# Tiles of x loaded from the Pool queue, weights loaded earlier, and memory columns copied one chain later, in a kernel of attention with recurrent memory plus a mixer MLP

## The chip, the cores and the metric

The kernel runs on one core of one Trainium2 chip. The metric is the device time of one execution in microseconds, as a median over several executions.

Ratios are the mean time of one kernel's fast runs over the mean time of the other's fast runs in the same rounds, so they are not quite the ratio of the medians that are quoted. They come with a 95% interval. Several chips were used: only kernels of one call share a chip and the runs of the kernel before.

## The reference, cut to what matters

Two branches read the same layer-normalised input, and the result is `x + A + B`.

```python
x = A_x                                     # (1, 2048, 1024), bf16
xn = _layernorm(x, axis=-1)
return x + _A_ref(xn, A_mem0, A_Wq, A_Wk, A_Wv, A_Wo, 32) + _B_ref(xn, B_w1, B_w2, B_w3, B_w4)

# A: for each of 64 segments of 32 tokens: 8 memory rows and the segment give q, k, v (32 heads of 128),
#    masked softmax, output projection; the first 8 output rows are the memory of the next segment
# B: h = gelu(layernorm(x) @ w1); four quarters of h shifted by -1, +1, -2, +2 tokens
#    x1 = x + shifted(h) @ w2 ;  x1 + gelu(layernorm(x1) @ w3) @ w4        # w3: 1024x3584
```

## The kernel before: the parts that matter

The kernel runs through stages one after another. Times are from its profile.

1. 0 to 72 us, "stage 1": 16 tiles of x (128 tokens each, 256 KB) are loaded, their statistics taken on VectorE, normalised, transposed (tiles 0 to 3 on TensorE, the others by a DMA transpose), and multiplied with w1. From tile 4 on two tiles are done at a time, with matmuls of 256 columns.
2. 72 to 127 us, the mixer: the product with w2, second layer norm, and a DMA transpose for each tile.
3. 127 to 531 us, the MLP: w3, gelu, w4, four times.
4. 531 us to the end: attention in 32 steps (4 blocks of 512 tokens, 8 groups of 4 heads). A step has 12 chains of 8 matmuls (4 for q, 4 for k, 4 for v). Work for the previous step's softmax is hooked between the chains.

Loads of x in stage 1. `nc.sync` is the SyncE queue, `nc.gpsimd` the Pool queue:

```python
def load_x(n):
    nc.sync.dma_start(xts[n][:], x_v[:, n, :])
...
load_x(0); load_x(1); load_w1(0); load_w1(2); load_x(2); load_w1(4); load_w1(6)   # (joined here)
for n in range(3, 8):
    load_x(n)
...
def ln_half(n, c):
    ...                                          # statistics on VectorE, then on Pool:
    nc.gpsimd.tensor_tensor(lnst[:, n, 2:4], ab[:], neghalf[:], op=ALU.pow)
...
def dma_trans(n):
    nc.sync.dma_start_transpose(xn2Ts[n // 2][:, n % 2, :, :], xn2s.pop(n)[:])
    if n + 4 < NT:
        load_x(n + 4)
    ...
def pe_trans(n):                                 # 8 matmuls with the identity, 2 copies on ScalarE
    ...
```

The part of attention that the change touches. `psO` is a buffer of two banks in PSUM, the memory that the matmuls write to. VectorE reads most of it (into `oX`), ScalarE the one memory column of each segment (into `oTm`):

```python
def values(s, m):
    ps = aux_tile([P, 4, 256], "B", "psO")
    for hh in range(4):
        nc.tensor.matmul(ps[:, hh, 0:TW], s.V[:, m, hh * P:(hh + 1) * P], BD[:, hh, :], start=True, stop=True)
    ...
    nc.vector.tensor_tensor(oX[...], p4[:, :, j0:4, 0:SEG], VM[...], op=ALU.add)
    nc.scalar.copy(oTm[:, hsl(s.hg), z:z + 4], p4[:, :, :, SEG])

for m in range(3):
    at(3 * m + 3, scores, p, m + 1)
    at(3 * m + 4, values, p, m)                  # hooked after chain 4, 7, 10
```

Of the kernel before, what the change touches and what calls it, by code (L numbers as in the profile page):

```python
# [25 lines left out]
NT = S // P  # L26
# [6 lines left out]
SEG = 32  # L33
# [30 lines left out]
def kernel(  # L64
# [16 lines left out]
    nc = tc.nc  # L81
    x_v = A_x[0].rearrange("(n p) d -> p n d", p=P)
# [49 lines left out]
    def mm_tile(name):  # L132
        return psum.tile([P, 512], F32, tag="mm", bufs=4, name=name)

    def aux_tile(shape, tag, name):
        return psum.tile(shape, F32, tag=tag, bufs=1, name=name)
# [16 lines left out]
    def load_w3(i):  # L153
        h, k = divmod(i, KT)
        nc.sync.dma_start(w3h[h][:, k, :], w3_v[:, k, h * FH * P:(h + 1) * FH * P])
# [7 lines left out]
    with ExitStack() as keepx:  # L163
        keep = keepx.enter_context(tc.tile_pool(name="keep", bufs=1))
        w2_sb = keep.tile([P, KT, D], BF16)
        xts = [keep.tile([P, D], BF16, name=f"x{n}") for n in range(NT)]
# [3 lines left out]
        with ExitStack() as p0:  # L170
# [6 lines left out]
            nc.scalar.activation(pre[:], fill[:, 0:1], ACTF.Gelu_apprx_tanh)  # L177

            def load_x(n):
                nc.sync.dma_start(xts[n][:], x_v[:, n, :])  # L180

            def load_w1(k0):
                nc.sync.dma_start(w1_sb[:, k0:k0 + 2, :], w1_v[:, k0:k0 + 2, :])
# [5 lines left out]
            load_x(2)  # L189
            load_w1(4)  # L190
            load_w1(6)
            for n in range(3, 8):
                load_x(n)

            def warm(c):
                ps = aux_tile([P, 512], "A", "psW")
# [5 lines left out]
            def ln_half(n, c):  # L202
                if c == 0:
                    sts[n] = ring.tile([P, 2, 6], F32, tag="st", name="st")
                nc.vector.bn_stats(sts[n][:, c, :], xts[n][:, c * 512:(c + 1) * 512])  # L205
                if c == 0:
                    return
                nc.vector.bn_aggr(lnst[:, n, 0:2], sts.pop(n)[:])
                ab = ring.tile([P, 2], F32, tag="ab", name="ab")
                nc.vector.tensor_scalar(ab[:, 0:1], lnst[:, n, 1:2], EPS, None, op0=ALU.add)  # L210
                nc.vector.tensor_scalar(ab[:, 1:2], ab[:, 0:1], EPS, lnst[:, n, 1:2], op0=ALU.mult, op1=ALU.add)
                nc.gpsimd.tensor_tensor(lnst[:, n, 2:4], ab[:], neghalf[:], op=ALU.pow)

            def ln_stats(n):
                ln_half(n, 0)
                ln_half(n, 1)
# [13 lines left out]

            def dma_trans(n):
                nc.sync.dma_start_transpose(xn2Ts[n // 2][:, n % 2, :, :], xn2s.pop(n)[:])
                if n + 4 < NT:
                    load_x(n + 4)
                if n == 8:
                    nc.sync.dma_start(m0[:], A_mem0[0])
                if 8 <= n < 12:
                    kk = slice(2 * (n - 8), 2 * (n - 7))
                    nc.sync.dma_start(w2_sb[:, kk, :], w2_v[:, kk, :])
                elif n >= 12:  # L240
                    load_w3(n - 12)
# [4 lines left out]
            def pe_trans(n):  # L246
                xn2 = xn2s.pop(n)
                ps = [mm_tile("psT")[:], mm_tile("psT")[:]]
                for h in range(2):
                    p3_ = ps[h].rearrange("p (k t) -> p k t", k=4)  # L250
                    for k in range(4):
                        nc.tensor.matmul(p3_[:, k, :], xn2[:, (4 * h + k) * P:(4 * h + k + 1) * P], ident[:], start=True, stop=True)
                    for q in range(0, 4, 2 if n == 0 else 4):
                        w = 2 if n == 0 else 4
                        nc.scalar.copy(xn2Ts[n // 2][:, n % 2, 4 * h + q:4 * h + q + w, :], p3_[:, q:q + w, :])
# [70 lines left out]
            normalise_x(2)  # L326
            ln_stats(6)
            ln_apply(5)
            dma_trans(5)
            single(3, 1)  # L330
            normalise_x(3)
            for g in range(2, NT // 2):
# [19 lines left out]
        with ExitStack() as p2:  # L352
            ring = p2.enter_context(tc.tile_pool(name="p2ring", bufs=4))
            for n in range(NT):
                x1 = ring.tile([P, D], F32, tag="x1", bufs=6)
                st = ring.tile([P, 2, 6], F32, tag="st")
                for ch in range(2):
                    ps = mm_tile("ps2")
                    for k in range(KT):
                        o = 2 + n * P + SH[k]  # L360
                        nc.tensor.matmul(ps[:], hTB[:, k, o:o + P], w2_sb[:, k, ch * 512:(ch + 1) * 512], start=(k == 0), stop=(k == KT - 1))  # L361
                    nc.vector.tensor_tensor(x1[:, ch * 512:(ch + 1) * 512], ps[:], xts[n][:, ch * 512:(ch + 1) * 512], op=ALU.add)
                    nc.vector.bn_stats(st[:, ch, :], x1[:, ch * 512:(ch + 1) * 512])
                mv = ring.tile([P, 2], F32, tag="mv")
                nc.vector.bn_aggr(mv[:], st[:])
                a = ring.tile([P, 1], F32, tag="a")
                nc.gpsimd.tensor_scalar(a[:], mv[:, 1:2], EPS, None, op0=ALU.add)
                r3 = ring.tile([P, 1], F32, tag="r3")
                nc.gpsimd.tensor_tensor(r3[:], a[:], neghalf[:, 0:1], op=ALU.pow)
                nm3 = ring.tile([P, 1], F32, tag="nm3")  # L370
                nc.gpsimd.tensor_scalar(nm3[:], mv[:, 0:1], r3[:], -1.0, op0=ALU.mult, op1=ALU.mult)
                xn3 = xts[n]
                nc.scalar.activation(xn3[:], x1[:], ACTF.Identity, bias=nm3[:], scale=r3[:])
                nc.gpsimd.dma_start(R1_v[:, n, :], x1[:])
                nc.sync.dma_start_transpose(xn3Ts[n // 4][:, n % 4, :, :], xn3[:])
                if n < 4:
                    load_w3(4 + n)
                elif n == 8:
                    load_qones()
                    load_causal()  # L380
                    load_mask40()

    attx = main.enter_context(ExitStack())
    with ExitStack() as p3:
        big = p3.enter_context(tc.tile_pool(name="p3big", bufs=1))
        ring = p3.enter_context(tc.tile_pool(name="p3ring", bufs=3))
        for i in range(8, 16):
            load_w3(i)
        w4t = []
        for c in range(7):  # L390
            t = big.tile([P, 4, D], BF16, name=f"w4_{c}")
# [142 lines left out]
        for tb in range(4):  # L534
# [14 lines left out]
            for j in range(4):  # L549
                n = tb * 4 + j  # L550
# [22 lines left out]
    oTm = abig.tile([P, H, NZ], BF16)  # L573
# [3 lines left out]
    def hsl(hg):  # L577
        return slice(4 * hg, 4 * hg + 4)
# [96 lines left out]
    def values(s, m):  # L675
        BD = s.u[m]
# [3 lines that stand above are left out]
        p4 = ps[:, :, 0:TW].rearrange("p h (j i) -> p h j i", i=W)  # L680
        j0 = 1 if (s.b == 0 and m == 0) else 0
        z = 7 + 16 * s.b + 4 * m
        nc.vector.tensor_tensor(  # L683
            oX[:, hsl(s.hg), m * P:(m + 1) * P].rearrange("p h (j i) -> p h j i", i=SEG)[:, :, j0:4, :],
            p4[:, :, j0:4, 0:SEG],
            VM[:, hsl(s.hg), z + j0:z + 4].unsqueeze(3).to_broadcast((P, 4, 4 - j0, SEG)), op=ALU.add)
        nc.scalar.copy(oTm[:, hsl(s.hg), z:z + 4], p4[:, :, :, SEG])  # L687

    QZ, PZ, VMZ, VZ = A["QZ"], A["PZ"], A["VMZ"], A["VZ"]

# [53 lines left out]
    def norm_recip(b, j):  # L744
        nc.vector.reciprocal(rms[b][:, j, :], rms[b][:, j, :])
# [93 lines left out]
    for i in range(NS):  # L839
        s = new_step(i)  # L840
        p = steps.get(i - 1)
        pp = steps.get(i - 2)
# [4 lines left out]
        def at(c, f, *a):  # L847
            hooks.setdefault(c, []).append((f, a))

        if pp is not None:  # L850
            at(1, values, pp, 3)
        if p is not None:
            at(0, scores, p, 0)
            for m in range(3):
                at(3 * m + 3, scores, p, m + 1)
                at(3 * m + 4, values, p, m)
        if 4 < s.hg and s.b + 1 < NB:
            for k in range(3 * s.hg - 15, min(3 * s.hg - 12, KT)):
                at(2 + 4 * (k % 3), make_xm, s.b + 1, (k,))
# [45 lines left out]
        if last:  # L905
            b = s.b
            load_Rt(b, 0)
            load_Rt(b, 1)
            hp = H - 4
            scores(s, 0)  # L910
            out_part(b, 0, 0, hp)
            values(p, 3)
            scores(s, 1)
            out_part(b, 1, 0, hp)
            values(s, 0)
            scores(s, 2)
            out_part(b, 2, 0, hp)
            values(s, 1)
            scores(s, 3)
            out_part(b, 0, hp, H)  # L920
            out_part(b, 1, hp, H)
            out_part(b, 3, 0, hp)
            values(s, 2)
            out_part(b, 2, hp, H)
            out_part(b, 3, hp, H)
            values(s, 3)
            norm_sums(b)
            for j in range(4):
                norm_recip(b, j)
            norm_apply(b)  # L930
            norm_add(b)
            out_chain(b, 4)
            out_chain(b, 5)
            verify()
            out_chain(b, 6)
            verdict()
            out_part(b, 7, 0, H, 2)
# [129 lines left out]
```

## Time and profile before

| | before |
|---|---|
| time, median of 3 | 1514.95 us (1514.44 to 1515.04) |
| span of the profiled execution | 1512.8 us |
| PE busy | 1502.9 us (99%) |
| start of stage 1's 256-column matmuls | 26.93 us |
| start of the mixer | 71.65 us |
| start of the MLP | 127.28 us |
| first q chain of attention | 530.83 us |
| first output projection (end of block 0) | 759.79 us |

The starts are those of the first matmul of each group in the timeline. The page of the kernel before begins so; a row of section 1 is engine, busy us, share of the span, number of instructions, and the last line is the chain of work that ended last, by engine.

```profile
span 1512.8 us, 24276 instructions
...
PE 1502.9 (99%) x9704; PEld 794.7 (53%) x9704; DVE 659.0 (44%) x1551; ACT 453.8 (30%) x1247; POOL 235.0 (16%) x652
...
PE 97%; DVE 1%; DMA 1%; ACT 0%; issue 0%; SPq 0%; POOL 0%; DVEq 0%
```

TensorE is the limit nearly all the time. So the change can only win what TensorE still loses. This is the list of waits of the kernel before, for TensorE alone (who waited for whom: us in total, times, the longest):

```profile
PE ps L278 <- DMA w_sb<-in_B_w_dram: 2.1, 3, 1.0
PE psW L198 <- DVE fill L175: 1.5, 1, 1.5
PE psQ L604 <- ACT V L628: 1.1, 2, 0.6
PE ps L265 <- DMA xn2T<-xn: 0.7, 1, 0.7
PE psT L252 <- DVE xn L227: 0.2, 1, 0.2
```

Line 1 is w1 not yet there. Line 4 is the DMA transpose of tile 5 (`xn2T` is the normalised, transposed tile). Line 3 is in attention. It comes from ScalarE's largest wait, here from the list of waits of all engines:

```profile
ACT oTm L687 <- DVE oX L683: 367.9, 128, 7.0
```

How a wait of ScalarE reaches TensorE can be read in the timeline of the kernel before around 681 us (start us, duration us, engine, line, operation, idle time before it and its end):

```profile
680.60 0.68 DVE L683 TENSOR_TENSOR oX<-psO,VM 128x512 bf16<-128x512 f32 x1
...
681.32 0.18 ACT L687 CAST oTm<-psO 128x16 bf16<-128x16 f32 x1 [2.71 <-DVE oX L683]
681.39 0.59 ACT L628 CAST V<-psV 128x512 bf16<-128x512 f32 x1
...
682.03 1.89 PE L604 MATMUL psQ<-xm,w 128*128 128x512 bf16 x8 [0.57 <-ACT V L628]
```

ScalarE stands 2.71 us in front of the small memory-column copy. The V copy behind it frees the PSUM buffer that the next q chain needs. TensorE therefore starts that chain late. The ordering between the two readers of `psO` is in the program: the Trainium skill, page "PSUM — Partial Sum Buffer", section "PSUM bank collisions raise a hardware error", says that two engines must not touch one PSUM bank on the same partitions at once, reads included. The trace agrees with it to this extent: all 128 copies waited for VectorE, 2.9 us each.

Around tile 5's transpose the chain in order of time of the kernel before (start us, us, what) has these pieces:

```profile
23.25 3.55 DMA xn2T<-xn
26.80 0.14 issue
26.93 3.65 PE ps L265 x32
```

And in the windows of the kernel before (stretch, its length, then for PE, PEld, DVE, ACT and POOL the busy us and the number of instructions, granted clock, mean busy share of the 16 DMA engines, GB/s moved), where DMA transposes and loads of x are both in SyncE's queue:

```profile
20.00:24.00 4.00, 4.00 (x77) 4.00 (x75) 3.86 (x11) 3.19 (x5) 2.36 (x4) 1.00 0.52 76
24.00:28.00 4.00, 3.33 (x60) 3.08 (x58) 3.44 (x11) 3.60 (x6) 1.32 (x3) 1.00 1.01 245
28.00:34.00 6.00, 6.00 (x70) 5.41 (x69) 4.79 (x14) 4.53 (x12) 3.39 (x6) 1.00 1.08 179
```

From 24 us on the DMA engines are fully busy (shares 1.01 and 1.08) and move 245 and 179 GB/s.

### The profile page before, as it was taken

To read this page: it belongs to the slowest core of one execution; us is meant where nothing else is said; L and a number is where in the kernel's file an instruction comes from. 1 tells how busy PE (TensorE), PEld (TensorE's weight loads), DVE (VectorE), ACT (ScalarE), POOL (GpSimd) and SP (SyncE) were. 2 spreads that over 40 slices of the span, in tenths; PEclk is the share of its full clock that TensorE was granted. 3 is DMA by queue.
4 is the path that set the end of the run, shared out by engine and by line. 5 is a ranking of instruction groups with operands and counts; after the bars stand their busy time and mean duration, and the time that the engine had idled before them with its cause. 6 is when DMAs were issued, how large, how long until landed. Compare 5 with 4: busy or idle time off the path is not lost.

```text
span 1512.8 us, 24276 instructions
## 1 busy us (share of the span) xinstructions
PE 1502.9 (99%) x9704; PEld 794.7 (53%) x9704; DVE 659.0 (44%) x1551; ACT 453.8 (30%) x1247; POOL 235.0 (16%) x652
## 2 busy tenths in 40 slices
PE   8999999999999999999999999999999999999998
PEld 7844444444444466666544544444544444454446
DVE  7283010010100226666622866731767640676653
ACT  5633202103012035444401344310443420344320
POOL 4152110111110211211201111110111110111100
PEclk9999999999999999999999999999999999999999
DMA  7699553553222454564522464421464431344211
GB/s 200 158 261 293 209 181 98 200 162 126 74 80 67 170 167 157 168 193 148 173 70 84 140 167 140 154 87 63 136 154 158 142 109 55 123 141 141 88 36 37
DMA packets 191062, 208.40 MB, mean 138 GB/s; under 512 B 51224, under 2 KB 158888, under 8 KB 190944
## 3 DMA queue, kind: packets, MB, share of 16 engines
q1 hardware_dynamic: 183696, 182.49, 39.9%
q0 software_dynamic: 7248, 24.31, 4.2%
q8 instruction: 78, 1.28, 0.4%
q14 instruction: 40, 0.33, 0.1%
HBM read 170.07 MB, written 25.17 MB: 129 GB/s over the span
## 4 chain that ended last, share of the span: by engine, by line
PE 97%; DVE 1%; DMA 1%; ACT 0%; issue 0%; SPq 0%; POOL 0%; DVEq 0%
PE psK L620 15%; PE psQ L604 15%; PE psP L776 15%; PE psV L627 14%; PE ps L539 13%; PE ps L557 13%; PE ps L361 4%; PE ps L265 3%; PE psS L649 2%; PE psO L679 2%; PE psM L636 1%; PE psY L798 1%; PE psvb L421 1%; DMA x<-in_A_x_dram 1%; PE psG L430 1%; DVE st L205 0%
## 5 line engine op out<-in xcount | busy, mean ns | idle before, releaser
L776 PE MATMUL psP<-wo_sb,oX 128*128 128x512 bf16 (+1 forms) x1056 | 222.9, 373 | 0.0
L653 ACT ACTIVATE ET<-psS 32x132 f32<-32x132 f32 x512 | 139.0, 272 | 187.4 <-PE psS L649 181.6
L557 PE MATMUL ps<-w,hT_all 128*128 128x512 bf16 x896 | 195.0, 379 | 0.0
L604 PE MATMUL psQ<-xT,w 128*128 128x512 bf16 x768 | 177.9, 379 | 0.0
L627 PE MATMUL psV<-w,xT 128*128 128x512 bf16 x768 | 177.6, 379 | 0.0
L620 PE MATMUL psK<-xT,w 128*128 128x512 bf16 x768 | 177.4, 379 | 0.0
L776 PEld LDWEIGHTS <-oX 128*128 128x128 bf16 x1056 | 102.8, 98 | 115.5
L620 PEld LDWEIGHTS <-w 128*128 128x128 bf16 x1280 | 121.3, 98 | 80.1
L604 PEld LDWEIGHTS <-w 128*128 128x128 bf16 x1024 | 97.0, 98 | 105.5 <-issue 1.3
L540 ACT ACTIVATE hT_all<-ps 128x512 bf16<-128x512 f32 x112 | 66.7, 597 | 283.9 <-PE ps L539 283.9
L557 PEld LDWEIGHTS <-hT_all 128*128 128x128 bf16 x896 | 87.2, 98 | 103.8
L687 ACT CAST oTm<-psO 128x16 bf16<-128x16 f32 x128 | 23.0, 179 | 367.9 <-DVE oX L683 367.9
L611 DVE TENSOR_TENSOR Q<-psQ,QM 128x512 bf16<-128x512 f32 (+1 forms) x128 | 85.3, 679 | 61.1 <-ACT Q L610 43.2
L655 DVE STREAM_TRANSPOSE EQ<-ET 128x128 f32<-128x128 f32 x128 | 39.8, 311 | 165.3 <-ACT ET L653 165.0
L627 PEld LDWEIGHTS <-xT 128*128 128x128 bf16 x768 | 72.1, 98 | 73.4
L670 POOL TENSOR_TENSOR BD<-ET,c_segone_sb 128x16 bf16<-128x16 f32 x128 | 33.7, 263 | 491.6 <-ACT ET L653 491.6
L539 PE MATMUL ps<-xn3T,w3a 128*128 128x512 bf16 x448 | 97.7, 379 | 0.0
L539 PE MATMUL ps<-xn3T,w3b 128*128 128x512 bf16 x448 | 97.7, 379 | 0.0
L668 DVE TENSOR_TENSOR BD<-PT,c_segone_sb 128x512 bf16<-128x512 bf16 x128 | 90.0, 703 | 4.5
L782 DVE TENSOR_TENSOR ot<-psP,Rt 128x512 bf16<-128x512 f32 (+1 forms) x33 | 22.2, 675 | 155.5 <-PE psP L776 154.7
L683 DVE TENSOR_TENSOR oX<-psO,VM 128x512 bf16<-128x512 f32 (+1 forms) x128 | 86.3, 675 | 7.4 <-PE psO L679 7.4
L621 ACT CAST K<-psK 128x512 bf16<-128x512 f32 (+1 forms) x160 | 78.7, 506 | 32.5 <-PE psK L620 31.9
(158 smaller groups left out, 1543.4 us busy)
## 6 DMA issues: line engine op xcount, KB each, us to landing
w<-in_A_Wq_dram SPq DMA_DIRECT2D x32, 1024.0 KB, 5.5
w<-in_A_Wk_dram SPq DMA_DIRECT2D x32, 1024.0 KB, 5.9
w<-in_A_Wv_dram SPq DMA_DIRECT2D x32, 1024.0 KB, 5.5
R_scratch<-x POOLq DMA_DIRECT2D x16, 512.0 KB, 3.9
R<-R_scratch SPq DMA_DIRECT2D x16, 512.0 KB, 7.3
chunk<-in_A_Wv_dram SPq DMA_DIRECT2D x8, 1024.0 KB, 6.6
R_scratch<-R POOLq DMA_DIRECT2D x16, 512.0 KB, 6.5
chunk<-in_A_Wo_dram SPq DMA_DIRECT2D x8, 1024.0 KB, 6.1
```

The source lines that it names most:

```text
L539: nc.tensor.matmul(ps[:], w3[:, k, (f % FH) * P:(f % FH + 1) * P], xn3Ts[tb][:, :, k, :], start=(k == 0), stop=(k == KT - 1))
L540: nc.scalar.activation(h3T[:, f, :], ps[:], ACTF.Gelu_apprx_tanh)
L557: nc.tensor.matmul(ps[:], h3T[:, f, j * P:(j + 1) * P], w4t[f // 4][:, f % 4, ch * 512:(ch + 1) * 512], start=(f == 0), stop=(f == FT - 1))
L604: nc.tensor.matmul(ps[:], w[:, k, hh * P:(hh + 1) * P], s.xm[:, k, 0:512], start=(k == 0), stop=(k == KT - 1))
L611: nc.vector.tensor_tensor(q3[:, j0:16, 0:SEG], p3_[:, j0:16, :], QM[:, 4 * s.hg + hh, z + j0:z + 16].unsqueeze(2).to_broadcast((P, 16 - j0 ...
L620: nc.tensor.matmul(ps[:, 0:c], w[:, k, hh * P:(hh + 1) * P], s.xm[:, k, h2 * c:(h2 + 1) * c], start=(k == 0), stop=(k == KT - 1))
L621: nc.scalar.copy(s.K[:, hh, h2 * c:(h2 + 1) * c], ps[:, 0:c])
L627: nc.tensor.matmul(ps[:], s.xm[:, k, m * P:(m + 1) * P], w[:, k, :], start=(k == 0), stop=(k == KT - 1))
L653: nc.scalar.activation(ET[q, :, :], ps[q, :, W * j:W * (j + 1)], ACTF.Exp, scale=SCALE)
L668: nc.vector.tensor_tensor(B4[:, :, :, 0:SEG], PT[:].unsqueeze(2).to_broadcast((P, 4, 4, SEG)), so.unsqueeze(3).to_broadcast((P, 4, 4, SEG) ...
L683: nc.vector.tensor_tensor(oX[:, hsl(s.hg), m * P:(m + 1) * P].rearrange("p h (j i) -> p h j i", i=SEG)[:, :, j0:4, :], p4[:, :, j0:4, 0:SE ...
L776: nc.tensor.matmul(ps[:, 0:w], oX[:, h, m * P:(m + 1) * P], wo_sb[:, h, cc], start=(h == 0), stop=(h == H - 1))
```

## The change

It has three parts, each meant to take a cause of waiting away.

- **x loads.** SyncE loads tiles 0 to 2 only. Pool issues the others as the statistics proceed, so that SyncE's queue is free for transposes. Tile 5 is transposed on TensorE.
- **w3.** The second half of w3 (`w3b`) is loaded within the mixer (12 of 16 pieces there, 4 of 16 before it), not after it.
- **Memory columns.** ScalarE copies them one chain after the values, when VectorE should be done.

```diff
             def load_x(n):
-                nc.sync.dma_start(xts[n][:], x_v[:, n, :])
+                (nc.sync if n < 3 else nc.gpsimd).dma_start(xts[n][:], x_v[:, n, :])
...
             load_w1(6)
-            for n in range(3, 8):
-                load_x(n)
...
                 nc.gpsimd.tensor_tensor(lnst[:, n, 2:4], ab[:], neghalf[:], op=ALU.pow)
+                for t in {0: (3,), 1: (4, 5), 2: (6, 7)}.get(n, (n + 5,)):
+                    if t < NT:
+                        load_x(t)
...                                             # in dma_trans
-                if n + 4 < NT:
-                    load_x(n + 4)
...
             ln_apply(5)
-            dma_trans(5)
+            pe_trans(5)
...                                             # mixer
-                if n < 4:
+                if n < 12:
                     load_w3(4 + n)
-                elif n == 8:
+                if n == 8:
...                                             # after the mixer
-        for i in range(8, 16):
-            load_w3(i)
...                                             # values
-        nc.scalar.copy(oTm[:, hsl(s.hg), z:z + 4], p4[:, :, :, SEG])
+        return lambda: nc.scalar.copy(oTm[:, hsl(s.hg), z:z + 4], p4[:, :, :, SEG])
...
+        def at_values(c, u, m):
+            later = []
+            at(c, lambda: later.append(values(u, m)))
+            at(c + 1, lambda: later.pop()())
...
-                at(3 * m + 4, values, p, m)
+                at_values(3 * m + 4, p, m)
...                                             # likewise values(pp, 3); values(...)() in the last step
```

More of the change, by code (lines that the diff above doesn't have):

```diff
@@ L848, in at @@
             hooks.setdefault(c, []).append((f, a))
+        def at_values(c, u, m):
+            later = []
+            at(c, lambda: later.append(values(u, m)))
+            at(c + 1, lambda: later.pop()())
         if pp is not None:
-            at(1, values, pp, 3)
+            at_values(1, pp, 3)
         if p is not None:
@@ L911 @@
             out_part(b, 0, 0, hp)
-            values(p, 3)
+            values(p, 3)()
             scores(s, 1)
             out_part(b, 1, 0, hp)
-            values(s, 0)
+            values(s, 0)()
             scores(s, 2)
             out_part(b, 2, 0, hp)
-            values(s, 1)
+            values(s, 1)()
             scores(s, 3)
@@ L922 @@
             out_part(b, 3, 0, hp)
-            values(s, 2)
+            values(s, 2)()
             out_part(b, 2, hp, H)
             out_part(b, 3, hp, H)
-            values(s, 3)
+            values(s, 3)()
             norm_sums(b)
```

## The prediction

> **What bounds the kernel.** TensorE: the page gives PE 1502.9 of 1512.8 us busy, and the chain of waits is 97% PE. Start-to-start intervals of neighbouring matmuls in the timeline (216 ns for 512 columns) show what can be regained: about 3.8 us in the first 27 us, 1.4 us between 560 and 737 us, under 0.2 us in every other stage (the 4 us after the last matmul stay). Over 2% (30 us) is out of reach.
>
> **Part 1: x tiles on Pool, tile 5 transposed on PE (first 27 us).** PE waits 2.1 us for w1 (list of waits; longest 1.0, at 10.65 us, for the third pair, landing at 11.78) and 0.7 us for the DMA transpose of tile 5 (issued 23.25).
> - Removed: tiles 3 to 7 leave SyncE's queue near w1's last pairs (windows: engines saturated from 8 to 13 us), and later tiles leave it between the transposes. Added: tile 3 enters Pool's queue at about 6.3 us, beside w1. "DMA: Bandwidth & Descriptors" (Trainium skill, section on SWDGE, HWDGE and iDMA) says that an engine round-robins between the two kinds of queue, so its 256 KB may pass the third pair. Net about 0.4 us gained (-0.5 to +1), capped because VectorE gets tile 2 only at 10.45 us.
> - Tile 5: 8 matmuls of 56 ns, +0.45 us, against an interval excess of 0.84 us. ScalarE's evacuations (0.54 us each) stand behind a normalisation ending at 26.0, so stage 1 starts about 26.7: 0.2 us gained.
> - Pool: 13 more issues of about 0.65 us; between its reciprocal roots it idles about 1.2 us: no visible delay.
>
> **Part 2: w3's second half inside the mixer.** Eight 0.46 MB loads move from 133-137 us to about 93-122 us. PE has no wait from 72 to 531 us; w3b, landed by 145.4, is first needed at about 151 us. Transposes lag more, but only tiles 0 to 3 are needed at 127 us. Value: 0.
>
> **Part 3: memory columns one chain later.** ScalarE's 128 copies wait 367.9 us in all for VectorE's oX, which reads the same PSUM tile; copies behind them stand. PE loses only at 681.26 and 707.51 us, 0.74 and 0.72 us (psQ waiting for a V copy queued behind a memory column copy that started at 681.32), and 0.10 at 630 us. One chain (3.45 us) later VectorE is nearly always done; the V copy runs at about 679.2. Gain 1.4 us; in the other blocks 0.
>
> **Sum.** 0.4 + 0.2 + 0 + 1.4 = 2.0 us. Predicted 1512.9 us, 8 times in 10 between 1510.9 and 1515.1. Faster by over 2%: 0.005; within 2%: 0.985; slower: 0.01.
>
> **What would show each step.** Right: the waits lose "PE psQ <- ACT V", 560 to 737 us shrinks by 1.4 us, ScalarE's wait for oX falls well under 100 us; 72 to 531 us keeps its length within 0.2 us though w3b lands some 20 us earlier; stage 1's 256-column matmuls start at about 26.3 (before: 26.93) without a wait for a DMA transpose. Wrong: a PE wait for xn2T from ScalarE near 26 us, a longer w1 wait, VectorE waiting for tiles 3 to 5 or Pool's roots, PE waiting for psO.
>
> **What would make it wrong.** Pool's loads taking DMA turns from tile 2 and w1 (front up to 1 us slower); w1's last pairs coming over 1 us sooner; scatter, 0.6 us over three runs.

## The result, and the profile after

| | before | changed |
|---|---|---|
| time, median of 6 each | 1514.39 us (1514.01 to 1515.04) | 1512.79 us (1512.03 to 1514.84) |
| ratio, 95% interval | | 0.9991 [0.9978, 1.0004] |
| start of stage 1's 256-column matmuls | 26.93 | 26.32 |
| start of the mixer | 71.65 | 73.05 |
| start of the MLP | 127.28 | 128.68 |
| first q chain | 530.83 | 532.22 |
| first output projection | 759.79 | 759.62 |

The interval of the ratio includes 1, so these runs alone do not show a gain. The medians differ by 1.6 us. The runs of the changed kernel scatter over 2.8 us, those of the kernel before over 1.0 us.

The traced execution of the changed kernel has a span of 1512.8 us, as before. That is long for this kernel: the spans of the six timed runs go from 1510.3 to 1513.1 us. Its table shows two things that cancel: 1.4 us lost up to the mixer and kept to the start of attention, and 1.56 us won in block 0 of attention (227.40 us from the first q chain to the first output projection, against 228.96). The list of waits of TensorE in the changed kernel:

```profile
PE ps L264 <- DMA xn2T<-xn: 1.8, 1, 1.8
PE ps L277 <- DMA w_sb<-in_B_w_dram: 1.5, 2, 1.1
PE psW L196 <- DVE fill L175: 1.5, 1, 1.5
PE psT L251 <- DVE xn L228: 0.4, 1, 0.4
PE ps L277 <- ACT xn2T L254: 0.2, 1, 0.2
```

The wait of psQ is gone. A new first line is there: 1.8 us for a DMA transpose. The chain in order of time of the changed kernel says which one:

```profile
26.92 8.66 DMA xn2T<-xn
35.58 0.14 issue
35.71 3.65 PE ps L264 x32
```

This is tile 7's transpose. In the kernel before it took 4.3 us (28.26 to 32.60), here 8.66. The windows of the changed kernel, as above:

```profile
20.00:24.00 4.00, 4.00 (x82) 4.00 (x80) 3.79 (x11) 3.17 (x6) 3.10 (x6) 1.00 0.86 170
24.00:28.00 4.00, 4.00 (x66) 3.78 (x62) 3.90 (x10) 4.00 (x8) 3.27 (x5) 1.00 0.76 170
28.00:34.00 6.00, 5.91 (x67) 5.10 (x64) 5.68 (x18) 5.00 (x13) 4.38 (x9) 1.00 1.15 111
```

From 28 to 34 us the DMA engines are as busy as before (1.15 against 1.08) and move less (111 GB/s against 179). The packet records of the trace agree: Pool's 4 KB packets took 0.37 to 0.73 us on average in each 2 us stretch from 26 to 34 us, against 0.17 to 0.19 from 20 to 26 us. The transposes' packets took 22 ns from 26 to 28 us, and 46 to 70 ns from 28 to 34 us.

In attention ScalarE waits less for VectorE, in the changed kernel's list of waits:

```profile
ACT oTm L684 <- DVE oX L680: 159.2, 121, 7.0
```

And the timeline of the changed kernel around the place shown above is:

```profile
680.46 0.59 ACT L625 CAST V<-psV 128x512 bf16<-128x512 f32 x1 [1.08 <-PE psV L624]
681.35 0.68 DVE L680 TENSOR_TENSOR oX<-psO,VM 128x512 bf16<-128x512 f32 x1
...
682.07 0.18 ACT L684 CAST oTm<-psO 128x16 bf16<-128x16 f32 x1
...
682.59 1.89 PE L601 MATMUL psQ<-xm,w 128*128 128x512 bf16 x7
```

The V copy now waits only for its own matmuls. The memory column follows it, and the q chain starts without a wait. (A "x7" where there are 8 is a record missing from the trace. This trace has 9586 matmuls on record, the one before 9704, although 8 were added.)

The mixer took 55.63 us in both kernels. From the MLP's start to attention it was 403.55 and 403.54 us. The w3 part changed nothing there.

### The profile page after: what moved, and what is told of

Same layout as the page of the kernel before. It is cut to its first block, busy times and chain, and to the rows that moved or that the text cites. A ratio compares the mean times of both kernels' runs of the same rounds, so it can differ in the third digit from the quotient of the medians.

```text
span 1512.8 us, 24179 instructions
## 1 busy us (share of the span) xinstructions
PE 1496.2 (99%) x9586; PEld 794.5 (53%) x9712; DVE 659.3 (44%) x1551; ACT 469.9 (31%) x1249; POOL 243.0 (16%) x665
## 4 chain that ended last, share of the span: by engine, by line
PE 97%; DVE 1%; DMA 1%; issue 1%; SPq 0%; POOL 0%
PE psK L617 15%; PE psP L773 15%; PE psQ L601 15%; PE psV L624 14%; PE ps L536 13%; PE ps L554 13%; PE ps L360 4%; PE ps L264 2%; PE psO L676 2%; PE psS L646 2%; PE psM L633 1%; PE psY L795 1%; DMA xn2T<-xn 1%; DVE st L203 1%; PE psvb L418 1%
## 5 line engine op out<-in xcount | busy, mean ns | idle before, releaser
L625 ACT CAST V<-psV 128x512 bf16<-128x512 f32 x128 | 75.1, 587 | 109.7 <-PE psV L624 99.7
```

Of the source, the lines that this page charges most:

```text
L625: nc.scalar.copy(s.V[:, m, :], ps[:])
```

## The experiments

Theories. **M**: the whole gain comes from the memory columns. **S**: loads of x in a second queue, beside SyncE's DMA transposes, make the transposes land late, and this costs what was hoped for in stage 1. Rivals are named where they are tested (one more, on the version with all loads up front, was not tested and is named there): the late transpose was a chance event (C), or came from transposing tile 5 on TensorE (T), or w3's part has an effect in combination (W).

Since TensorE works without a gap from its first 256-column matmul to the mixer if nothing is late, the length of this stretch is the sharpest measure. It is 44.72 to 44.77 us undisturbed. All runs in one table ("tile 7" is its DMA transpose; a median pair is kernel and before, same call):

| kernel | who loads tiles 8 to 15 | tile 7: issue, landing, us between | PE waits for DMA transposes | stretch | medians | ratio, 95% |
|---|---|---|---|---|---|---|
| before (first trace) | SyncE, between transposes | 28.26, 32.60, 4.3 | 0.7 (tile 5) | 44.72 | | |
| changed (first trace) | Pool | 26.92, 35.58, 8.7 | 1.8 | 46.73 | 1512.79 / 1514.39 | 0.9991 [0.9978, 1.0004] |
| memory columns alone | SyncE, between | 27.58, 31.52, 3.9 | 1.1 (tile 5) | 44.72 | 1512.52 / 1514.22 | 0.9986 [0.9972, 0.9999] |
| x loads and tile 5 alone | Pool | 27.31, 36.39, 9.1 | 2.1 | 47.00 | 1515.30 / 1514.22 | 1.0004 [0.9990, 1.0018] |
| w3 alone | SyncE, between | 27.60, 32.50, 4.9 | 0.7 (tile 5) | 44.72 | 1513.92 / 1514.22 | 0.9995 [0.9981, 1.0009] |
| changed, again | Pool | 26.60, 33.67, 7.1 | 0.3 | 45.21 | 1513.44 / 1514.22 | 0.9995 [0.9982, 1.0009] |
| tile 5 on PE alone | SyncE, between | 27.95, 32.55, 4.6 | none | 44.76 | 1512.43 / 1514.36 | 0.9988 [0.9974, 1.0002] |
| Pool loads alone | Pool | 27.39, 34.31, 6.9 | 0.6 (tile 5) | 44.73 | 1514.77 / 1514.36 | 1.0003 [0.9989, 1.0017] |
| changed, tiles 8 on to SyncE | SyncE, between | 27.36, 31.50, 4.1 | none | 44.77 | 1512.55 / 1514.36 | 0.9989 [0.9976, 1.0003] |
| changed, all x up front on SyncE | SyncE, before any transpose | 26.75, 30.33, 3.6 | none | 44.76 | 1511.13 / 1514.36 | 0.9978 [0.9965, 0.9992] |
| w3 and memory columns | SyncE, between | 27.64, 31.95, 4.3 | 1.1 (tile 5) | 44.72 | 1512.23 / 1513.57 | 0.9991 [0.9977, 1.0005] |
| all x up front, tile 5 by DMA | SyncE, before | 26.80, 30.32, 3.5 | none listed | 44.72 | 1511.95 / 1513.57 | 0.9990 [0.9976, 1.0003] |
| changed, tiles 8 on to ScalarE | ScalarE's queue | 26.61, 33.11, 6.5 | none | 45.29 | 1513.17 / 1513.57 | 0.9999 [0.9985, 1.0012] |
| all x up front, w3 as before | SyncE, before | 25.92, 29.80, 3.9 | none | 44.76 | 1511.25 / 1513.87 | 0.9984 [0.9971, 0.9998] |

All outputs are right.

### Call 1: the three parts one by one, and the changed kernel again

**Memory columns alone.** The hunks of `values`, `at_values` and their calls applied to the kernel before:

```diff
-                at(3 * m + 4, values, p, m)
+                at_values(3 * m + 4, p, m)
```

> Only the memory columns are copied one chain later; loads as before. Theory M (all the net gain is this part): about 1.5 us faster than before (ratio 0.9990), the list of waits loses PE psQ <- ACT V, and the stretch from the first psQ matmul to the first psP matmul falls from 228.96 to about 227.4 us. Rival N (the gain comes from the x loads or w3, and the attention stretch only shrank by chance): no change within 0.3 us.

Measured: 1.7 us under before in the medians, and the interval excludes 1. TensorE's waits have no psQ line any more, and the stretch from the first q chain to the first output projection is 227.64 us. ScalarE's wait in its list of waits is as in the changed kernel:

```profile
ACT oTm L687 <- DVE oX L683: 160.4, 121, 7.0
```

Theory M holds: this part alone gives as much as the whole change (1.7 and 1.6 us in the medians).

**x loads and tile 5 alone.** The hunks of `load_x`, `ln_half`, `dma_trans` and `pe_trans(5)`:

```diff
-                nc.sync.dma_start(xts[n][:], x_v[:, n, :])
+                (nc.sync if n < 3 else nc.gpsimd).dma_start(xts[n][:], x_v[:, n, :])
```

> Only the x tiles on Pool and tile 5 transposed on PE. Theory S (Pool's loads of tiles 8 to 15 share the DMA engines with the DMA transposes and delay tile 7's): stage 1 starts near 26.3 (0.6 earlier than before), then PE waits 1 to 3 us for a DMA transpose near 33.6, the mixer starts 0.4 to 2 us later than 71.65, and the kernel is 0.5 to 2 us slower than before. Rival C (the wait in the profile of the changed kernel was a chance event or came with the other parts): no such wait, mixer at about 71.0, kernel 0.6 us faster.

Measured: the wait is there again (2.1 us), tile 7 lands 9.1 us after issue, and the mixer starts at 73.86 us, 2.2 us later than before. The start of the 256-column matmuls, 26.86 us, was not 0.6 us early as expected. The median is 1.1 us over before, with an interval that includes 1. The chain in order of time of this run:

```profile
27.31 9.07 DMA xn2T<-xn
```

**w3 alone.** The load hunks of the mixer:

```diff
-                if n < 4:
+                if n < 12:
                     load_w3(4 + n)
```

> Only w3's second half moved into the mixer. Both theories: no PE wait, start of the first w3 chain within 0.2 us of before's 127.28, time within 0.3 us of before; the last mixer transposes land about 15 us later (before 135.86).

Measured: no time of its own that these runs can tell (0.3 us in the medians, interval includes 1). The MLP starts at 126.62 us, 0.66 earlier than in the first trace of before. This is not w3's doing: the mixer already starts 0.66 us earlier, at 70.99, with stage 1 unchanged. This was the first sign that the start of stage 1 scatters by that much from one execution to the next. The transposes of the mixer did land later, the last one at 146.28 us (10.4 us later, 15 were expected). The loads as a whole gained nothing, though. In the changed kernel the last piece of w3 landed at 146.63 us, against 145.44 before (its MLP starts 1.4 us later), and the last piece of w4 at 174.12 against 165.35. SyncE issued the pieces of w3's second half among the mixer's transposes, from 98.08 to 139.59 us, against 133.39 to 136.84 before, and the DMA engines were busy already (0.85 before, 0.94 in the changed kernel's mixer). So the pieces and the transposes changed places: the first piece landed at 104.33 us instead of 137.19, the last one no earlier.

**The changed kernel again.**

> The changed kernel once more. Theory S: the PE wait for a DMA transpose near 33.6 us is there again, 1 to 3 us, and the time is 1 to 2 us under before. Rival C: no wait there, and the profiled execution is 2 us shorter than the first one (about 1511 us span).

Measured: the wait is there, but only 0.3 us. Tile 7 still took 7.1 us. The median was 0.8 us under before, less than expected, and the span of the profiled execution was 1511.0 us, which is what C had said: stage 1 started at 25.93 us and lost 0.5 us in its stretch, not 2.0. TensorE waited 1.8, 2.1 and 0.3 us for tile 7 in the three traces with Pool's loads and tile 5 on TensorE, and never in a trace without them, and the transpose was late each time, so chance (rival C) is not the cause. But the size varies from one execution to the next. The timed runs of the changed kernel scatter by 2.8 and 2.6 us, those of the memory columns alone by 1.1. This fits, but does not prove it: the version with w3 and memory columns, which has no such wait in its trace, scattered by 2.3 us.

### Call 2: which part of the x change

**Tile 5 on PE alone**, with `load_x(9)` kept in its place:

```diff
             ln_apply(5)
-            dma_trans(5)
+            pe_trans(5)
+            load_x(9)
```

> The kernel before, with tile 5 transposed on PE and nothing else (all x loads on SyncE, in their old places). Theory S: no wait for tile 7's transpose; from the first 256-column matmul of stage 1 to the mixer's start 44.7 us as in before (47.0, 46.7 and 45.2 in the three runs with Pool's loads), first 256-column matmul 0 to 0.5 us earlier than before, time 0 to 0.5 us under before. Rival T (PE's transpose of tile 5, by moving PE's demand for tiles 6 and 7, makes the wait): that stretch is 45.2 or longer and PE waits for a DMA transpose near 33.6.

Measured: no late transpose (4.6 us) and a stretch of 44.76. Rival T falls. The time was 1.9 us under before in the medians, more than expected, with an interval that just includes 1. The trace shows little of it up to the mixer, which starts at 70.89 us, against 70.97, 70.99 and 71.04 in three other traces with the old stage 1. It shows 0.56 us more after the last matmul: from there to the end of the span are 3.73 us, against 4.29 before. That time differs by version: 3.73 to 3.74 us in the three traces with tile 5 on TensorE and all x loads on SyncE, 4.28 to 4.31 in the five with tile 5 by DMA and all x loads on SyncE, 4.15 to 4.57 in the six others. Why it does was not looked into. So how much this half is worth stays open.

**Pool loads alone**, tile 5 transposed by DMA as before:

```diff
-            pe_trans(5)
+            dma_trans(5)
```

(against the version with x loads and tile 5.)

> The kernel before, with tiles 3 to 15 loaded by Pool and tile 5 still transposed by the DMA queue. Theory S: transposes of tiles 5 to 7 land late (over 6 us after issue for tile 7, against 4.3 before), PE waits in sum 1 to 4 us for DMA transposes before 36 us, time 0.5 to 3 us over before. Rival T: no such wait near 33 us, stretch from the first 256-column matmul to the mixer 44.7 us.

Measured: the transposes of tiles 6 and 7 are late (7.9 and 6.9 us), as S says. The cost was smaller than S expected: TensorE waited 0.6 us, for tile 5. Tile 7 landed at 34.31, just before TensorE came to it at about 34.5, because TensorE had itself started late (27.15). That start has a long wait for w1 in it, 1.8 us, as in the version with x loads and tile 5. The time was 0.4 us over before, interval including 1.

**Tiles 8 to 15 back on SyncE.** Everything else as changed:

```diff
-                (nc.sync if n < 3 else nc.gpsimd).dma_start(xts[n][:], x_v[:, n, :])
+                (nc.gpsimd if 3 <= n < 8 else nc.sync).dma_start(xts[n][:], x_v[:, n, :])
...                                             # and load_x(n + 4) back in dma_trans
```

> The changed kernel with tiles 8 to 15 back on SyncE behind the transposes; tiles 3 to 7 stay on Pool, tile 5 stays on PE, w3 and memory columns as changed. Theory S: tile 7's transpose lands within 4.5 us of its issue, stretch from the first 256-column matmul to the mixer 44.7 us, time about 2 us under before, 0.5 to 1.5 under the changed kernel. Rival T: stretch stays at 45.2 to 47.

Measured: tile 7 lands 4.1 us after its issue, no wait, stretch 44.77. So Pool's loads of tiles 8 to 15 are what delays the transposes; moving them changed their queue and their times together. The gain of 1.8 us in the medians is about that of the memory columns.

**All x loads up front on SyncE.** If the loads are the trouble only while transposes run, they can be done earlier: SyncE and the DMA engines are idle from 16 to 20 us in the kernel before (0.00 share in the windows).

```diff
-                (nc.sync if n < 3 else nc.gpsimd).dma_start(xts[n][:], x_v[:, n, :])
+                nc.sync.dma_start(xts[n][:], x_v[:, n, :])
...
             load_w1(6)
+            for n in range(3, NT):
+                load_x(n)
...                                             # no load_x in ln_half
```

> The changed kernel with all x loads on SyncE right after w1's, so that they are done (about 2.1 MB more at 400 KB/us from 14 us on) when the first DMA transpose is issued near 20 us. Theory S: transposes of tiles 4, 6 and 7 land 2.5 to 3.5 us after issue, no PE wait for a DMA transpose, stretch 44.7 us, time about 2 to 2.5 us under before and the fastest of all so far. Rival T: stretch 45.2 to 47 all the same.

Measured: 1511.13 us, 3.2 us under before, the fastest median of all and more than expected. The interval excludes 1. Tile 7's transpose took 3.6 us. TensorE's list of waits in this version has no DMA transpose any more:

```profile
PE psW L198 <- DVE fill L175: 1.5, 1, 1.5
PE psT L250 <- DVE xn L227: 1.2, 1, 1.2
PE ps L276 <- DMA w_sb<-in_B_w_dram: 1.0, 1, 1.0
PE ps L276 <- ACT xn2T L253: 0.2, 1, 0.2
```

Its windows show where the loads went. From 14 to 20 us the engines move 369 GB/s, and from 20 us on they have little but transposes to do:

```profile
14.00:20.00 6.00, 6.00 (x111) 6.00 (x109) 5.68 (x17) 4.47 (x8) 2.50 (x4) 1.00 1.00 369
20.00:24.00 4.00, 4.00 (x84) 4.00 (x82) 3.79 (x12) 3.17 (x8) 1.74 (x4) 1.00 0.60 85
24.00:28.00 4.00, 4.00 (x54) 3.70 (x52) 3.86 (x10) 4.00 (x7) 2.36 (x4) 1.00 0.39 73
28.00:34.00 6.00, 6.00 (x70) 5.42 (x68) 5.72 (x17) 4.55 (x11) 3.02 (x5) 1.00 0.81 119
```

Where the gain over the kernel before lies can be added up from the two traces, whose spans differ by 3.5 us: 1.39 us in the start of the 256-column matmuls (25.54 against 26.93), nothing in the stretch (44.76 against 44.72), 1.56 us in block 0 of attention, and 0.55 us after the last matmul. So this version avoids the late transpose of tile 7, but that is no gain over the kernel before, in which TensorE never waited for tile 7. The earlier start is not shown to come from the up-front loads either. In this version, in the one below with w3 as before, and in tile 5 on PE alone, TensorE's last wait for w1 ended at 10.82, 10.05 and 11.41 us, and the start followed 14.72 us later in all three; w1 is loaded before the loads that were moved. A rival thus stays untested: that what this version wins beyond the memory columns comes from tile 5 on TensorE, which alone gave 1.9 us in the medians, and not from the up-front loads. The run that would settle it, memory columns and tile 5 on TensorE with the old x loads, was not made.

### Calls 3 and 4: a control, the kind of queue, and the best version

**w3 and memory columns**, the x part left out:

```diff
-                (nc.sync if n < 3 else nc.gpsimd).dma_start(xts[n][:], x_v[:, n, :])
+                nc.sync.dma_start(xts[n][:], x_v[:, n, :])
...                                             # and all other x and pe_trans(5) hunks undone
```

> The changed kernel without its first part: w3 in the mixer and memory columns later, x loads and tile 5's transpose as before. Theory S with M: as the memory columns alone, 1.4 to 1.7 us under before; no PE wait for tile 7's transpose; mixer and the w3/w4 stages unchanged in length (55.63 and 403.55 us). Rival W (w3's loads in the mixer cost something that shows only with the others): 1 us or less under before, with one of those two stretches longer.

Measured: 1.3 us under before in the medians, just short of the expected 1.4 to 1.7. The mixer took 55.63 us and the stretch from the MLP to attention 403.55 us, exactly as elsewhere. Rival W has no support in the stages.

**All x up front, tile 5 by DMA.**

```diff
             ln_apply(5)
-            pe_trans(5)
+            dma_trans(5)
```

> As the version with all x loads up front (1511.13 us), but tile 5 transposed by the DMA queue again. If tile 5's late landing in the kernel before (issued 23.25, stage 1 held until 26.93) came only from tile 8's load beside it: its transpose now lands before PE wants it, PE saves 8 transposes (0.45 us), first 256-column matmul at about 25.1 instead of 25.54, time about 0.4 us under 1511.13. If it came from the transpose's own duration (3.2 us for tile 4 in the quiet): PE waits 0.3 to 0.8 us at about 25, and the time is the same or up to 0.4 us longer.

Measured: tile 5's transpose, issued at 22.15, lands 3.1 us later at 25.21. TensorE comes at about 25.1 and has an interval excess of 0.25 us there. So the start is 25.35 us, between the two expectations. In the kernel before, tile 5's transpose was issued at 23.25, behind tile 8's load, and landed at 26.80: without tile 5 on TensorE, this is the wait that is shorter with up-front loads (0.25 us here, 0.7 to 1.1 us in the four traces with the old stage 1). The time was 1.6 us under before in the medians, with an interval that includes 1; the version with w3 and memory columns was 1.3 us under, so the medians do not show what the up-front loads add here. This version ran on another chip than the previous one, whose start was 25.54, and a third version with the same stage 1 as that had 24.77. The scatter is larger than the difference, and whether transposing tile 5 on TensorE pays stays open.

**Tiles 8 to 15 from ScalarE's queue.** This asks whether it is Pool's queue or any second queue:

```diff
-                (nc.sync if n < 3 else nc.gpsimd).dma_start(xts[n][:], x_v[:, n, :])
+                (nc.sync if n < 3 else nc.gpsimd if n < 8 else nc.scalar).dma_start(xts[n][:], x_v[:, n, :])
```

> The changed kernel with tiles 8 to 15 issued by ScalarE, that is on a hardware queue of its own, at nearly the times at which Pool issued them. Theory S1 (any second queue beside the transposes slows them): tile 7's transpose lands 6 to 9 us after issue, PE waits 0.3 to 2 us near 33 us, time as the changed kernel's. Theory S2 (only Pool's queue, with its 4 KB packets, does it): tile 7 lands within 4.5 us of issue, no such wait, time about 1 us under the changed kernel.

Measured: tile 7's transpose took 6.5 us, while two loads that ScalarE had issued at 26.3 and 26.7 were in flight. So it need not be Pool's queue: S1 is supported by the landing. TensorE did not wait for it, since it landed at 33.1, just in time. It lost 0.4 us at about 37.5 us to ScalarE instead, which had stopped to issue loads. The view of the tile xn2T, cut to what was issued between 26 and 29 us (that is tile 7), compares four cases; the second line of each is the time from issue to landing. First the changed kernel:

```profile
L233 SPq DMA_TRANSPOSE xn2T<-xn x1: 1239/1239/1239, 26.9 to 26.9; - x1
DMA to landing us min/median/max: 8.7/8.7/8.7
```

Then the version that loads from ScalarE's queue:

```profile
L233 SPq DMA_TRANSPOSE xn2T<-xn x1: 1233/1233/1233, 26.6 to 26.6; - x1
DMA to landing us min/median/max: 6.5/6.5/6.5
```

Then the version with tiles 8 to 15 back on SyncE:

```profile
L233 SPq DMA_TRANSPOSE xn2T<-xn x1: 1232/1232/1232, 27.4 to 27.4; - x1
DMA to landing us min/median/max: 4.1/4.1/4.1
```

And the version with all loads up front:

```profile
L232 SPq DMA_TRANSPOSE xn2T<-xn x1: 2301/2301/2301, 26.8 to 26.8; - x1
DMA to landing us min/median/max: 3.6/3.6/3.6
```

The last number of each pair falls from 8.7 over 6.5 and 4.1 to 3.6 us. What changes is in which queue the loads of other tiles are, and with it when they run: four of Pool's loads overlap tile 7's transpose in time in the changed kernel, two of ScalarE's in the second case, two on record of SyncE's in the third, none in the last. So their number alone does not explain it: with two loads in flight it took 6.5 us beside a second queue and 4.1 with one queue. Whether Pool's queue is worse than ScalarE's (8.7, 9.1, 7.1, 6.9 against 6.5) can't be told from one trace of the latter.

**All x up front, w3 as before.** A second run of the best stage 1, and a last test of w3:

```diff
-                if n < 12:
+                if n < 4:
                     load_w3(4 + n)
...                                             # and pieces 8 to 15 after the mixer again
```

> As the version with all x loads up front on SyncE (1511.13 us, tile 5 on PE, memory columns later), but w3's second half loaded after the mixer as before. Theory S with M and w3 neutral: the same time within 0.5 us, 2.5 to 3.3 us under before of the same rounds, no PE wait for a DMA transpose, mixer 55.6 us. Rival W (w3's part gives or costs something in this combination): over 0.5 us away from that.

Measured: 1511.25 us, 2.6 us under before, interval excluding 1. So the gain of the up-front loads with tile 5 on TensorE and the memory columns is seen twice, on two chips, and w3's part adds nothing that shows.

## Why the prediction was right or wrong, point by point

- **The total, 1512.9 us (1510.9 to 1515.1).** Measured 1512.79. It was right in size, and the view that TensorE leaves only a few microseconds to win is what made it so. Its sum was not right in its parts, and so the close hit is partly luck: the 0.6 us of part 1 were not seen, and the second set of runs of the changed kernel was 0.8 us under before. The gain in the same rounds was 1.6 us, not 2.0.
- **Part 3, "Gain 1.4 us".** Right. The wait of psQ is gone in every run that has this part. Block 0 shrank by 1.56 us in the changed kernel and by 1.32 with this part alone. The mechanism is the one given: the V copy no longer stands behind the memory column. The V copy began at 680.46 us, which is 679.07 on the clock of the kernel before (attention started 1.39 us later); 679.2 was predicted. One size was off: "ScalarE's wait for oX falls well under 100 us". It fell from 367.9 to 159.2. The wrong step was "One chain (3.45 us) later VectorE is nearly always done". The 3.45 us that I took from the chain of waits are 16 matmuls, which is two chains. One chain is 8 matmuls of 216 ns, 1.73 us. As an estimate, 128 copies moved by 1.73 us would leave 367.9 - 221.4 = 146.5 us of waiting, close to the 159.2 measured (121 waits of 1.3 us). This cost TensorE nothing, because the copies that matter to it are no longer behind that wait.
- **Part 2, "Value: 0".** Right for the time. Wrong in a detail: "w3b lands some 20 us earlier". It landed complete at 146.63 us, 1.2 later than before. Its last piece was issued at 139.59 us, behind the mixer's transposes, and not by 122 as predicted. I had seen the transposes lag during the first four loads in the mixer, and did not carry that lag over to the loads themselves.
- **Part 1, "Net about 0.4 us gained" at w1.** Not seen. TensorE waited for w1 1.5, 2.3, 1.1, 2.0, 1.0 and 1.4 us in the six traces with Pool's loads of tiles 3 to 7, and 0.8 to 1.2 us in the four later traces with x loads as before. The 2.1 us of the first trace, on which the estimate rested, is above those. The page "DMA: Bandwidth & Descriptors", section "SWDGE vs HWDGE vs iDMA", which I had used for the risk that Pool's tile 3 passes w1, agrees with the order of landing: tile 3 landed at 12.48 us, before w1's fourth pair at 12.91.
- **Part 1, "stage 1 starts about 26.7: 0.2 us gained", with the sum "start at about 26.3".** It was 26.32 in the first trace, but this shows little: with the old stage 1 the start was 26.93, 26.25, 26.27 and 26.32, and with the x part 26.32, 26.86 and 25.93.
- **The step that failed.** The prediction looked for the damage of Pool's loads at tile 2, w1 and Pool's reciprocal roots. It said of the later tiles only that taking them out of SyncE's queue is good for the transposes. The runs showed the opposite: beside another queue's loads tile 7's transpose took 6.5 to 9.1 us instead of 3.5 to 4.9, and TensorE waited 0.3 to 2.1 us for tile 7 in the three traces with the whole x part. That DMA engines take turns between queues stood in the prediction. I applied it to the loads and not to the transposes.

What is shown: which part gives the changed kernel's gain, that loads of tiles 8 to 15 in a second queue delay the transposes, and that earlier loads on the same queue avoid it. The two versions with these loads and tile 5 on TensorE beat both kernels: all ten of their runs, 1510.33 to 1511.88 us, lie under the fastest of the 11 runs of the changed kernel (1512.03), though on other chips in part. The third version with these loads, tile 5 by DMA, does not (1511.55 to 1512.26 us, 1.6 us under before, interval including 1). What is not shown: whether the up-front loads or tile 5 on TensorE give what the two win beyond the memory columns. What is argued only: why the engines move less in that mixture. The packet times show that both kinds of packet get slower, not the reason.

## What to carry to other kernels

When TensorE is busy 99% of the time, list its waits and expect no more than their sum; here one small copy that stood in front of a PSUM-freeing copy was worth 1.3 to 1.7 us, and no reordering of loads was shown to be worth more. Be wary of moving plain loads to a second queue to make room for DMA transposes that something waits for: here that slowed the transposes. Loads put ahead of the transposes, in a stretch where the DMA engines are idle, left tile 7's transpose at 3.5 to 3.9 us; that takes memory for all tiles at once. Writing a load earlier in the program need not make it land earlier: the last piece of w3 stood behind transposes in SyncE's queue and landed no sooner.

## What the Trainium skill lacked or had wrong

- Page "DMA: Bandwidth & Descriptors", section "Rules for kernel authors", says that a transpose next to ordinary DMAs needs nothing. As a rule for correctness nothing here speaks against it. For time it lacks a warning: the same DMA transpose of 128 x 1024 bf16 (tile 7's) landed 3.5 to 4.9 us after issue with the other loads of that time on its own queue or already done, and 6.5 to 9.1 us with loads on Pool's or ScalarE's queue beside it.
- The same section says that spreading DMAs over SyncE, ScalarE and Pool doesn't help bandwidth. Here it hurt: 111 GB/s from 28 to 34 us in the changed kernel at a busy share of 1.15, against 179 GB/s at 1.08 before. The share of the DMA engines is thus no measure of what they move.
- Page "DMA: Bandwidth & Descriptors", section "DMA Transpose (X-bar)", gives constraints and no duration; what the page has elsewhere is a bandwidth, not the time of one transpose. The runs show 3.1 to 3.9 us from issue to landing for 256 KB when little else is in flight (tile 5 and tile 7 with all x loads up front).
